# First layer of a two-block transformer stack: statistics of the tokens on VectorE at every second key unit, transposes inside the key units, no statistics on ScalarE, first copy in halves

## Chip, cores and metric

The kernel runs on one core of a Trainium2 chip. The metric is the device time of one execution in microseconds (us). "Before" and "after" are the two versions of the kernel. Times are medians of several executions, with the lowest and highest in brackets. A profile is one execution, and its span is about 1.8 us shorter than that execution's device time.

## The reference

Four layers on 2048 tokens of width 1024: linear attention (A), gated bilinear block (B), A, B, each on a layer norm of its input and added to it. Only the start of the first A layer matters here.

```python
def _A_ref(x, wqkv, wo):
    B, S, D = x.shape
    H = 32; Dh = D // H
    qkv = (x @ wqkv).reshape(B, S, 3, H, Dh).transpose(2, 0, 3, 1, 4)
    q, k, v = qkv[0], qkv[1], qkv[2]
    phi = lambda t: jnp.where(t > 0, t + 1, jnp.exp(t)) + 1e-6
    pq, pk = phi(q), phi(k)
    kv = jnp.einsum("bhsd,bhse->bhde", pk, v)
    z = jnp.einsum("bhsd->bhd", pk)
    # ... cut: num / den, times wo
x = A_x
x = x + _A_ref(_layernorm(x, axis=-1), A_wqkv, A_wo)
# ... cut: B, A, B in the same way
```

## The kernel before

The tokens are 16 tiles of 128, in four groups of four. For each tile the kernel takes mean and variance, normalises, transposes (the matmuls of this kernel read the tokens with D on the partitions), and runs two key units of eight 128x512 matmuls each. `phi` of a unit is one exponential on ScalarE and two passes on VectorE. The program emits each engine's instructions in the order of the calls below, and the traces show them run in that order (in after, an offset on Pool that was ready at 20.5 us ran at 22.88 us, behind one emitted earlier), so this order is the schedule. In the calls, `bn(t, h)` is `bn_stats` of half h of tile t, `ln_stats(t)` both halves and `moments(t)`, and `ln_apply(t, ...)` the normalisation, all on VectorE but for Pool's two steps in `moments`.

```python
def moments(t):                       # after two bn_stats of 512 columns each
    mv = small.tile([P, 2], F32, tag="mv", bufs=2 * TPG, name="mv")
    nc.vector.bn_aggr(out=mv[:], in_=stat[t][0][:])
    ve = small.tile([P, 1], F32, tag="ve", name="ve")
    nc.gpsimd.tensor_scalar(out=ve[:], in0=mv[:, 1:2], scalar1=1e-5, scalar2=None, op0=ALU.add)
    rstd = small.tile([P, 1], F32, tag="rstd", bufs=2 * TPG, name="rstd")
    nc.gpsimd.tensor_tensor(out=rstd[:], in0=ve[:], in1=mhalf[:], op=ALU.pow)
    stat[t] = (mv, rstd)

def ln_stats_act(t, xn):              # the same statistics by two ScalarE passes over the tile
    add = small.tile([P, 2], F32, tag="add", name="add")
    nc.scalar.activation(out=xn, in_=X[:, t, :], func=ACT.Identity, accum_out=add[:, 0:1])
    # ... cut: Pool makes -mean
    nc.scalar.activation(out=xn, in_=X[:, t, :], func=ACT.Square, bias=mv[:, 1:2], accum_out=add[:, 1:2])
    # ... cut: Pool makes mean, variance, rstd

def ln_apply_act(t, xn):
    mv, rstd = stat.pop(t)
    off = small.tile([P, 1], F32, tag="off", name="off")
    nc.gpsimd.tensor_scalar(out=off[:], in0=mv[:, 0:1], scalar1=rstd[:], scalar2=-1.0,
                            op0=ALU.mult, op1=ALU.mult)
    nc.scalar.activation(out=xn, in_=X[:, t, :], func=ACT.Identity, scale=rstd[:], bias=off[:])

def tx(xn, t, slot):                  # transpose by DMA
    tl = t % TPG
    nc.sync.dma_start_transpose(out=xT[slot][:, :, tl * P:(tl + 1) * P], in_=xn)

def tx_pe(xn, t):                     # transpose on TensorE, copy on ScalarE
    pt = psum.tile([P, KD, P], BF16, tag="mm", bufs=8, name="pt")
    for k in range(KD):
        nc.tensor.transpose(out=pt[:, k, :], in_=xn[:, k * P:(k + 1) * P], identity=ident[:])
    nc.scalar.copy(out=xT[t // TPG][:, :, t % TPG * P:(t % TPG + 1) * P], in_=pt[:])

def phi(ps, dst):
    e = work.tile([P, NB], BF16, tag="e", bufs=3, name="e")
    nc.scalar.activation(out=e[:], in_=ps[:], func=ACT.Exp)
    nc.vector.tensor_scalar(out=e[:], in0=e[:], scalar1=1.0, scalar2=1e-6, op0=ALU.min, op1=ALU.add)
    nc.vector.scalar_tensor_tensor(out=dst, in0=ps[:], scalar=1.0 + 1e-6, in1=e[:], op0=ALU.add, op1=ALU.max)

# first layer; k[2 * t + n] is the key unit of tile t, half n
def norm(t):
    ln_apply_act(t, xn_a[t])
    tx(xn_a[t], t, t // TPG)

bn(0, 0); bn(0, 1); moments(0)
bn(1, 0); ln_apply(0, xn_a[0]); tx_pe(xn_a[0], 0)
bn(1, 1); moments(1)
bn(2, 0); ln_apply(1, xn_a[1]); tx_pe(xn_a[1], 1)
bn(2, 1); moments(2)
bn(3, 0); ln_apply(2, xn_a[2])
bn(3, 1); moments(3); ln_stats(4)
k[0](); tx_pe(xn_a[2], 2); ln_apply(3, xn_a[3])
k[2](); tx_pe(xn_a[3], 3)
ln_stats_act(5, xn_a[5])
# ... cut: the rest of group 1, in the manner of the loop below
for g in range(2, NG):                # units of group g-1 with the norms of group g
    t = g * TPG
    u = k[8 * g - 8:8 * g]
    ln_stats(t)
    ln_stats_act(t + 1, xn_a[t + 1])
    u[0](); norm(t);     ln_stats(t + 2)
    u[1](); norm(t + 1); ln_stats(t + 3)
    u[2](); norm(t + 2)
    u[3](); norm(t + 3)
    do(u[4:])                         # ... cut: loads of input tiles 12 to 15 in between
do(k[8 * NG - 8:])
```

All matmul outputs rotate through eight PSUM buffers. Sixteen matmuls on zeros run while the first inputs arrive, to warm the clock up (in before's trace they take 634 ns each at first and 379 ns at the end).

## Time and profile before

| | before |
|---|---|
| device time | 1644.73 us (1644.15 to 1646.07, 3 runs); with a later fourth run 1644.59 |
| the profiled execution | 1646.92 us, span 1645.1 |
| TensorE busy | 1629.4 us, 99% |
| first key unit, first unit of tile 4, end of key units | 9.45, 28.59, 79.04 us |
| from the end of the key units to the end | 1566.06 us |

The first lines are of the page of before. The second line has busy time, share of the span and number of instructions per engine; the third has the granted TensorE clock in 40 equal slices, in tenths.

```profile
span 1645.1 us, 18292 instructions
...
PE 1629.4 (99%) x7696; PEld 744.8 (45%) x7696; DVE 641.3 (39%) x1042; ACT 270.4 (16%) x452; POOL 57.7 (4%) x159
...
PEclk9999999999999999999999999999999999999999
```

At this scale there is nothing to see: 16 us are idle in 1645, and a clock that was half for some 7 us does not show in a slice of 41 us. The timeline of TensorE of before does show it. Columns: start in us, length in us, engine, line, operation, output and inputs, count; in brackets the idle time before and what ended it. L214 is the transposes, L233 the key units.

```profile
9.45 1.89 PE L233 MATMUL ps<-W_74,xT_70 128*128 128x512 bf16 x8
14.19 0.62 PE L214 MATMUL pt<-ident,W_76 128*128 128x128 bf16 x8 [2.85 <-DVE W_76 L194]
...
17.77 0.62 PE L214 MATMUL pt<-ident,W_76 128*128 128x128 bf16 x8 [1.23 <-DVE W_76 L194]
...
44.76 1.90 PE L233 MATMUL ps<-W_74,xT_72 128*128 128x512 bf16 x8 [2.20 <-DMA xT_72<-XW]
...
62.81 3.59 PE L233 MATMUL ps<-W_74,xT_73 128*128 128x512 bf16 x8 [4.07 <-DMA xT_73<-D_84]
66.20 2.64 PE L233 MATMUL ps<-W_75,xT_73 128*128 128x512 bf16 x8
68.68 1.89 PE L233 MATMUL ps<-W_74,xT_73 128*128 128x512 bf16 x8
...
79.04 1.03 PE L245 MATMUL ps<-H,W_76 128*128 128x512 bf16 x4
```

A unit starts 1.727 us after the one before it when nothing waits. Three kinds of hole stand out: a start in which TensorE waits for VectorE's normalisation, a hole of 2.2 us before group 2 and one of 4.1 us before group 3. After the last, two units are slow. The stretches of before say why (columns: stretch, length, TensorE busy and count, granted clock, DMA share, GB/s):

```profile
62.00:64.00 2.00, 1.19 (x3) 0.50 0.10 18
64.00:66.00 2.00, 2.00 (x6) 0.50 0.68 131
66.00:68.00 2.00, 2.00 (x6) 0.57 0.68 131
68.00:70.00 2.00, 2.00 (x11) 1.00 1.00 165
```

The clock was half. It had fallen at about 60.9 us (the stretches 60.50:61.00 and 61.00:61.50 show 0.89 and 0.50). The timeline of ScalarE of before shows what made group 2 late. L180 and L183 are the two statistics passes of tile 9, L223 an exponential, L203 a normalisation.

```profile
33.07 1.07 ACT L180 ACTIVATE XW<-X 128x1024 bf16<-128x1024 bf16 x1
34.02 0.21 ACT L180 ACTIVATION_READ_ACCUMULATOR XW<-X 128x1 f32 x1
37.88 1.15 ACT L183 ACTIVATE XW<-X,mv 128x1024 bf16<-128x1024 bf16 x1 [3.65 <-POOL mv L182]
...
39.03 0.58 ACT L223 ACTIVATE e<-ps 128x512 bf16<-128x512 f32 x1
40.34 1.24 ACT L203 ACTIVATE XW<-X,off,rstd 128x1024 bf16<-128x1024 bf16 x1 [0.73 <-POOL off L201]
```

ScalarE stood still for 3.65 us between the two passes. The step of Pool that it waited for (L182) was in Pool's queue behind the variance of tile 8 (L167), which VectorE had not finished:

```profile
36.65 0.23 POOL L167 TENSOR_SCALAR ve<-mv 128x1 f32<-128x1 f32 x1 [7.56 <-DVE mv L165]
...
37.62 0.23 POOL L182 TENSOR_SCALAR mv<-add 128x1 f32<-128x1 f32 x1
```

The exponential at 39.03 us, for which VectorE waited 3.1 us, could not pass.

### The profile page before, as it was taken

The numbers are of one execution on the slowest core, as the hardware profiler recorded it, in microseconds if no ns is written. First come the engines' busy times: TensorE is split into PE (matmuls) and PEld (weight loads), VectorE is DVE, ScalarE is ACT, GpSimd is POOL, SyncE is SP. The second block draws the span as 40 slices with busy tenths as digits, with TensorE's granted clock in tenths as the row PEclk, the third lists the DMA queues.
The fourth block names the chain that finished last, engine by engine and source line by source line (L and its number), as shares of the span: only waits on it lengthen the run. The fifth ranks groups of instructions, "written<-read, shape, count | busy, mean of one in ns | idle before, by whom it ended". The sixth has DMA issues, their size and how long they took to land.

```text
span 1645.1 us, 18292 instructions
## 1 busy us (share of the span) xinstructions
PE 1629.4 (99%) x7696; PEld 744.8 (45%) x7696; DVE 641.3 (39%) x1042; ACT 270.4 (16%) x452; POOL 57.7 (4%) x159
## 2 busy tenths in 40 slices
PE   8899999999999999999999999999999999999999
PEld 3344544444444444444444444444444444444444
DVE  5789963211321321111677889531132113211111
ACT  4522301100110110011023223011011101100110
POOL 2100000000000000000200000000000000000000
PEclk9999999999999999999999999999999999999999
DMA  5602719630641363041460126394225406421400
GB/s 166 167 14 39 199 34 316 194 102 2 178 154 51 101 175 109 0 154 51 103 154 1 32 60 165 105 330 154 67 68 173 157 23 172 151 75 63 154 4 23
DMA packets 245009, 182.58 MB, mean 111 GB/s; under 512 B 100544, under 2 KB 235712, under 8 KB 244928
## 3 DMA queue, kind: packets, MB, share of 16 engines
q1 hardware_dynamic: 244928, 181.43, 38.2%
q8 instruction: 60, 0.98, 0.2%
q14 instruction: 21, 0.17, 0.0%
HBM read 153.09 MB, written 4.19 MB: 96 GB/s over the span
## 4 chain that ended last, share of the span: by engine, by line
PE 96%; DVE 1%; issue 1%; DMA 1%; ACT 1%; POOL 0%; SPq 0%; ACTq 0%; DVEq 0%
PE ps L348 47%; PE ps L365 24%; PE ps L233 11%; PE ps L334 7%; PE ps L245 7%; DVE H L225 0%; DMA X<-in_A_x_dram 0%; PE ps L310 0%; PE ps L319 0%; DVE st L161 0%; SPq L103 0%; ACT e L223 0%; DMA xT_73<-D_84 0%; DVE e L224 0%; POOL rstd L169 0%
## 5 line engine op out<-in xcount | busy, mean ns | idle before, releaser
L352 DVE TENSOR_TENSOR H<-gs,ps 128x512 bf16<-128x512 f32 x224 | 154.1, 688 | 575.1 <-PE ps L348 570.6
L351 ACT COPY gs<-ps 128x512 f32<-128x512 f32 x224 | 131.3, 586 | 1039.4 <-PE ps L348 1039.4
L365 PEld LDWEIGHTS <-H 128*128 128x128 bf16 x1848 | 178.5, 98 | 208.7
L367 DVE TENSOR_TENSOR X<-X,ps 128x512 bf16<-128x512 bf16 (+1 forms) x66 | 44.3, 671 | 319.7 <-PE ps L365 319.7
L223 ACT ACTIVATE e<-ps 128x512 bf16<-128x512 f32 x128 | 75.5, 595 | 164.7 <-PE ps L233 157.3
L348 PEld LDWEIGHTS <-W_75 128*128 128x128 bf16 x640 | 62.6, 98 | 75.5
L348 PEld LDWEIGHTS <-W_74 128*128 128x128 bf16 x640 | 62.6, 98 | 75.5
L348 PEld LDWEIGHTS <-W_77 128*128 128x128 bf16 x576 | 56.4, 98 | 67.9
L348 PEld LDWEIGHTS <-xT_73 128*128 128x128 bf16 x576 | 56.4, 98 | 67.9
L348 PEld LDWEIGHTS <-W_76 128*128 128x128 bf16 x576 | 56.4, 98 | 68.0
L348 PEld LDWEIGHTS <-xT_72 128*128 128x128 bf16 x576 | 56.4, 98 | 68.0
L161 DVE BATCH_NORM_STATS2 st<-X 128x6 f32<-128x512 bf16 x122 | 77.5, 675 | 5.7 <-DMA X<-in_A_x_dram 5.7
L348 PE MATMUL ps<-xT_71,W_74 128*128 128x512 bf16 x320 | 75.6, 379 | 0.0
L348 PE MATMUL ps<-xT_70,W_74 128*128 128x512 bf16 x320 | 75.6, 379 | 0.0
L348 PE MATMUL ps<-xT_71,W_75 128*128 128x512 bf16 x320 | 75.6, 379 | 0.0
L348 PE MATMUL ps<-xT_70,xT_73 128*128 128x512 bf16 x320 | 75.6, 379 | 0.0
L348 PE MATMUL ps<-xT_71,W_76 128*128 128x512 bf16 x320 | 75.6, 379 | 0.0
L348 PE MATMUL ps<-xT_71,W_77 128*128 128x512 bf16 x320 | 75.6, 379 | 0.0
L348 PE MATMUL ps<-xT_70,W_75 128*128 128x512 bf16 x320 | 75.6, 379 | 0.0
L348 PE MATMUL ps<-xT_70,xT_72 128*128 128x512 bf16 x320 | 75.6, 379 | 0.0
L365 PE MATMUL ps<-D_80,H 128*128 128x512 bf16 (+2 forms) x264 | 66.0, 373 | 0.0
L365 PE MATMUL ps<-D_78,H 128*128 128x512 bf16 (+2 forms) x264 | 66.0, 373 | 0.0
(125 smaller groups left out, 1825.7 us busy)
## 6 DMA issues: line engine op xcount, KB each, us to landing
W_74<-in_B_w_gate_dram SPq DMA_DIRECT2D x20, 1024.0 KB, 5.2
W_75<-in_B_w_up_dram SPq DMA_DIRECT2D x20, 1024.0 KB, 7.4
W_76<-in_B_w_gate_dram SPq DMA_DIRECT2D x18, 1024.0 KB, 5.2
W_77<-in_B_w_up_dram SPq DMA_DIRECT2D x18, 1024.0 KB, 7.0
xT_72<-in_B_w_gate_dram SPq DMA_DIRECT2D x18, 1024.0 KB, 5.2
xT_73<-in_B_w_up_dram SPq DMA_DIRECT2D x18, 1024.0 KB, 7.2
X<-in_A_x_dram SPq DMA_DIRECT2D x16, 256.0 KB, 4.9
H<-in_A_wo_dram SPq DMA_DIRECT2D x4, 1024.0 KB, 7.2
```

What stands on the lines that cost most here:

```text
L161: nc.vector.bn_stats(out=stat[t][0][:, c, :], in_=X[:, t, c * NB:(c + 1) * NB])
L223: nc.scalar.activation(out=e[:], in_=ps[:], func=ACT.Exp)
L233: nc.tensor.matmul(out=ps[:], lhsT=xt[:, k, tl * P:(tl + 1) * P], rhs=w[:, k, :], start=(k == 0), stop=(k == KD - 1))
L245: nc.tensor.matmul(out=ps[:], lhsT=xn_a[t][:, j * P:(j + 1) * P], rhs=pk[t][:, n * NB:(n + 1) * NB], start=(t == 0), stop=(t == NT - 1))
L334: nc.tensor.matmul(out=ps[:], lhsT=xT[t // TPG][:, c, tl * P:(tl + 1) * P], rhs=KVo[n][:, c, :], start=(c == 0), stop=(c == KD - 1))
L348: nc.tensor.matmul(out=ps[:], lhsT=w[:, k, j * P:(j + 1) * P], rhs=xT[g % 2][:, k, :], start=(k == 0), stop=(k == KD - 1))
L351: nc.scalar.copy(out=gs[:], in_=gp[:])
L352: nc.vector.tensor_tensor(out=hT[:, f, :], in0=gs[:], in1=up[:], op=ALU.mult)
L365: nc.tensor.matmul(out=ps[:, 0:hi - lo], lhsT=hT[:, f, tl * P:(tl + 1) * P], rhs=wd[f][:, cols], start=(f == 0), stop=(f == KF - 1))
L367: nc.vector.tensor_tensor(out=X[:, t, cols], in0=X[:, t, cols], in1=ps[:, 0:hi - lo], op=ALU.add)
```

## The change

The intent: statistics on VectorE only, one tile per two units, early enough that the DMA transposes land before their units; the transposes of tiles 1 to 3 inside units, so that TensorE does not wait for the copies; input tiles 3 to 11 loaded at once; first copy in two halves, so that the first four matmuls start earlier; three warm-up matmuls fewer. Cut to its core (`k_mm(t, n, ...)` emits the matmuls of one key unit and returns what `phi` needs; `txp(t)` is the transposes of tile t, which `mid` puts inside a unit):

```diff
-    for t in range(3, 2 * TPG):
+    for t in range(3, 3 * TPG):
         load_x(t)
-    for i in range(16):
+    for i in range(13):
         nc.tensor.matmul(out=zps[:], ...)
-    def ln_stats_act(t, xn): ...           # cut: dropped
-        nc.scalar.copy(out=xT[t // TPG][:, :, ...], in_=pt[:])
+        parts = 2 if t == 0 else 1
+        for ks in (slice(i * KD // parts, (i + 1) * KD // parts) for i in range(parts)):
+            nc.scalar.copy(out=xT[t // TPG][:, ks, ...], in_=pt[:, ks, :])
-    def proj(t, w, dst):
+    def proj_mm(t, w, mid=None, at=KD // 4):
         for k in range(KD):
+            if k == at and mid is not None:
+                mid()                      # the next tile's transposes
             nc.tensor.matmul(out=ps[:], ...)
-            # cut: the order of before's first layer
+            bn(0, 0); bn(0, 1); moments(0)
+            bn(1, 0); bn(1, 1); ln_apply(0, xn_a[0]); tx_pe(xn_a[0], 0)
+            moments(1); bn(2, 0); ln_apply(1, xn_a[1])
+            bn(2, 1); moments(2)
+            u = k_mm(0, 0, txp(1))
+            ln_apply(2, xn_a[2]); phi(*u)
+            u = k_mm(1, 0, txp(2))
+            ln_stats(3); bn(4, 0); ln_apply(3, xn_a[3]); bn(4, 1); moments(4)
+            phi(*u)
+            ln_apply(4, xn_a[4]); tx(xn_a[4], 4, 1)
+            units = [(2, 0), (0, 1), (1, 1), (3, 0), (2, 1), (3, 1)]
+            units += [(t, n) for t in range(TPG, NT) for n in range(2)]
+            ready = []
+            for i, (t, n) in enumerate(units):
+                u = k_mm(t, n, txp(3), KD // 2) if i == 1 else k_mm(t, n)
+                late = ready
+                ready = [4 + (i + 4) // 2 if i > 1 else 5 + i] if i < 2 or (i % 2 == 0 and i <= 18) else []
+                for x in ready:
+                    ln_stats(x)
+                phi(*u)
+                for x in late:
+                    norm(x)
+                if i == 2:
+                    for x in range(3 * TPG, NT):
+                        load_x(x)
```

## The prediction

> **What bounds the kernel.** The page gives TensorE 1629.4 us busy of 1645.1 (99%); the chain that ended last is TensorE for 96%. The list of TensorE's waits holds 12.8 us, all before 63 us. The timeline shows where: 1.2, 2.9 and 1.2 us before the transposes of tiles 1, 2, 3 (behind VectorE's normalisation), 2.2 us at 42.6 us and 4.1 us at 58.7 us (behind the DMA transposes of groups 2 and 3). After the 4.1 us hole the stretches show a granted clock of 0.50 until about 67.5 us: two units took 3.39 and 2.48 us instead of 1.73, 2.4 us more. The Trainium skill, "TensorE: Matmul & The Clock Gate", Part 1, says that an idle window of about 3.4 us halves the clock; holes of 2.9 (no drop) and 4.1 us (drop) agree.
>
> The 32 key units need 32 x 1.727 = 55.3 us; they end at 79.0 us. So 23.8 us of this stage is start, transposes, holes and slow clock. From there on TensorE never waits.
>
> **What the change does.**
> - VectorE no longer runs tile 3's statistics (input lands at 12.97 us) ahead of normalising tile 2. That was the 2.9 us hole.
> - Statistics on ScalarE go for three tiles: 1.06 + 0.19 + 1.15 + 0.19 us each, plus Pool steps between. Behind them VectorE waited 3 us for an exponential at 36.5 and 54.7 us. VectorE gets three more statistics (1.5 us each).
> - Statistics are spread one per two units: 1.51 + 2 x 0.93 = 3.37 us of VectorE per 3.45 us of TensorE.
> - Transposes of tiles 1 to 3 stand inside units, so ScalarE's 1.01 us copies hide. The first copy in halves lets the first unit start about 0.45 us earlier. Three warm-up matmuls go (they ended at 7.3 us, after tile 0 was ready at 6.6).
>
> **Walk with trace durations (estimate).** Tile 0 normalised 6.7, transposed 7.3, half copied 7.9, first unit 8.0. Tile 1 ready 8.9 (its apply stands behind tile 2's arrival, 7.66): wait 0.5, unit ends 10.7. Second unit, wait 0.2, ends 13.1; third 14.8. Fourth waits 0.4 for tile 3 (input 12.97, normalised 16.0), ends 17.4. From there units run back to back: tile 4 is needed at 24.3, lands 21.5; tile 5 27.8 against 25.5; tile 7 34.7 against 31.5 to 33; later ones 4 us or more to spare. VectorE lags TensorE by up to 6 us (3 to 4 units), within eight PSUM buffers, and catches up after the last statistics near 52 us. Key units end near 65.7 us instead of 79.0: 13.3 us off the critical path. 1644.7 - 13.3 = 1631.4; I add 0.4 for small slips.
>
> **Time:** 1631.8 us, 8 in 10 within 1628.5 to 1637. Faster by over 2%: 0.01; within 2%: 0.98; slower: 0.01.
>
> **What would show it.** No TensorE wait over 1 us after 10 us; clock 1.00 after warm-up; the first matmul of the next stage (line 245 before) near 65.7 us; VectorE about 97% busy from 18 to 52 us with phi 5 to 6 us behind its unit; everything later unchanged, 13 us earlier.
>
> **What would make it wrong.** VectorE is nearly full: 2 us more lag and the DMA transposes of tiles 4, 5, 7 come late and open holes again. Thirteen warm-ups may not release the clock: in the trace they sped up only near 5.9 us; then the first units run at half clock, about 2 us more.

## More of the kernel before

All ordinary loads and DMA transposes are issued by SyncE, in program order.

Tile 8's own offset, whose inputs were ready at 37.53 us, stood in Pool's queue behind tile 9's steps and ran at 40.04; so ScalarE normalised tile 8 at 40.34 us, its transpose was issued at 41.60, and TensorE got it at 44.76.

## The result, and the profile after

After takes 1634.24 us (1633.99 to 1634.62, 4 runs); before, in the same rounds and its earlier ones, 1644.59 us. The ratio is 0.9936, with a 95% interval of 0.9919 to 0.9953. The gain is 10.4 us.

The same lines of the page of after:

```profile
span 1632.4 us, 18134 instructions
...
PE 1618.0 (99%) x7543; PEld 743.6 (46%) x7693; DVE 645.2 (40%) x1052; ACT 262.2 (16%) x440; POOL 57.0 (3%) x152
...
PEclk9999999999999999999999999999999999999999
```

The trace of after has 7543 matmul records where 7693 weight loads ran; some matmul records are missing, so TensorE's busy time of the two pages is not compared. The timeline of TensorE of after (L199 the transposes, L222 the key units, L240 the next stage; adjoining units are merged):

```profile
1.17 4.77 PE L153 MATMUL zps<-xT 128*128 128x512 bf16 x13 [1.17 <-DVE xT L150]
...
8.00 0.60 PE L222 MATMUL ps<-W,xT 128*128 128x512 bf16 x2 [0.68 <-ACT xT L202]
...
11.37 4.05 PE L222 MATMUL ps<-W,xT 128*128 128x512 bf16 x17
15.75 0.62 PE L199 MATMUL pt<-ident,W 128*128 128x128 bf16 x8 [0.33 <-DVE W L179]
16.21 18.44 PE L222 MATMUL ps<-W,xT 128*128 128x512 bf16 x82
35.47 31.04 PE L222 MATMUL ps<-W,xT 128*128 128x512 bf16 x141 [0.82 <-DMA xT<-W]
66.56 1.89 PE L240 MATMUL ps<-H,W 128*128 128x512 bf16 x8
```

The big holes are gone. One new wait is left, 0.82 us at 35.47 us, for the DMA transpose of tile 7. Tile 4's first unit starts at 23.98 us (16.21 us plus half a unit plus four units of 1.727), 4.6 us earlier than before. The key units end at 66.56 us, 12.5 us earlier. What follows takes 1565.84 us, against 1566.06: nothing was given back later.

Yet the timed medians are only 10.4 us apart. The profiled execution of before took 1646.92 us, 2.3 us above its median; that of after, 1634.15 us, lies on its median. So 2.1 us of the 12.5 are a question about the kernel before, and the wait for tile 7 is a question about the kernel after.

Two traces bear on the second. First, Pool in after: L167 and L169 are the variance steps of a tile, L186 the offset with which ScalarE normalises it.

```profile
19.61 0.22 POOL L167 TENSOR_SCALAR ve<-mv 128x1 f32<-128x1 f32 x1 [2.11 <-DVE mv L165]
19.91 0.57 POOL L169 TENSOR_TENSOR rstd<-ve,mhalf 128x1 f32<-128x1 f32 x1
21.93 0.22 POOL L167 TENSOR_SCALAR ve<-mv 128x1 f32<-128x1 f32 x1 [1.45 <-DVE mv L165]
22.23 0.57 POOL L169 TENSOR_TENSOR rstd<-ve,mhalf 128x1 f32<-128x1 f32 x1
22.88 0.27 POOL L186 TENSOR_SCALAR off<-mv,rstd 128x1 f32<-128x1 f32 x1
```

Tile 5's inputs were ready at 20.5 us, but its offset ran at 22.88: the program emits it after tile 6's statistics, so it stood behind tile 6's variance, which waited for VectorE. The Trainium skill ("Perfetto Trace Analysis", section "Per-engine timelines", in the note on TensorE) says that ScalarE, VectorE and GpSimd run strictly in order of arrival; this trace agrees, with 2.4 us lost. Second, the issues of SyncE in after (L193 a DMA transpose, L103 a load):

```profile
18.11 10.06 SPq L193 DMA_TRANSPOSE xT<-W  x3
28.22 2.00 SPq L103 DMA_DIRECT2D X<-in_A_x_dram  x4
30.33 1.39 SPq L193 DMA_TRANSPOSE xT<-W  x1
```

Tile 7 was normalised at 28.5 us. Its transpose was issued at 30.33, behind four loads of 256 KB, and landed 5.1 us later (the chain of waits), where transposes of this stage usually took 3.1.

### The profile page after: what moved, and what is told of

It reads as the page before. It is cut to its first block, busy times and chain, and to the rows that moved or that the text cites. A ratio compares the mean times of both kernels' runs of the same rounds, so it can differ in the third digit from the quotient of the medians.

```text
span 1632.4 us, 18134 instructions
## 1 busy us (share of the span) xinstructions
PE 1618.0 (99%) x7543; PEld 743.6 (46%) x7693; DVE 645.2 (40%) x1052; ACT 262.2 (16%) x440; POOL 57.0 (3%) x152
## 4 chain that ended last, share of the span: by engine, by line
PE 97%; DMA 1%; issue 1%; DVE 1%; SPq 0%; POOL 0%; ACT 0%; ACTq 0%
PE ps L343 47%; PE ps L360 24%; PE ps L222 12%; PE ps L240 7%; PE ps L329 7%; DMA X<-in_A_x_dram 0%; PE ps L305 0%; PE ps L314 0%; SPq L103 0%; DMA xT<-W 0%; DVE st L161 0%; PE ps L266 0%; POOL rstd L169 0%; DVE H L212 0%; ACT e L210 0%
## 5 line engine op out<-in xcount | busy, mean ns | idle before, releaser
L343 PE MATMUL ps<-xT,W 128*128 128x512 bf16 x2380 | 525.8, 379 | 2.8
L360 PE MATMUL ps<-D,H 128*128 128x512 bf16 (+2 forms) x1811 | 385.9, 372 | 1.8
L343 PEld LDWEIGHTS <-W 128*128 128x128 bf16 x2432 | 238.0, 98 | 286.9
L343 PE MATMUL ps<-xT,xT 128*128 128x512 bf16 x1134 | 250.6, 379 | 1.0
L343 PEld LDWEIGHTS <-xT 128*128 128x128 bf16 x1152 | 112.7, 98 | 135.9
L222 PEld LDWEIGHTS <-xT 128*128 128x128 bf16 x1024 | 99.6, 98 | 121.7 <-DMA xT<-W 2.0
L222 PE MATMUL ps<-D,xT 128*128 128x512 bf16 x501 | 114.8, 379 | 0.5
L222 PE MATMUL ps<-W,xT 128*128 128x512 bf16 x501 | 110.9, 379 | 2.0 <-DMA xT<-W 0.8
L329 PE MATMUL ps<-D,xT 128*128 128x512 bf16 x502 | 110.3, 379 | 0.5
L329 PEld LDWEIGHTS <-xT 128*128 128x128 bf16 x512 | 50.1, 98 | 60.4
L240 PE MATMUL ps<-H,W 128*128 128x512 bf16 x248 | 59.9, 379 | 0.5
L167 POOL TENSOR_SCALAR ve<-mv 128x1 f32<-128x1 f32 x64 | 15.0, 234 | 1295.9 <-DVE mv L165 1295.9
L321 DVE TENSOR_TENSOR X<-X,ps 128x512 bf16<-128x512 bf16 x64 | 42.1, 679 | 32.8 <-PE ps L329 32.8
L212 DVE SCALAR_TENSOR_TENSOR pq<-ps,e 128x512 bf16<-128x512 f32 x64 | 44.3, 692 | 2.5
```

The source lines that it names most:

```text
L222: nc.tensor.matmul(out=ps[:], lhsT=xt[:, k, tl * P:(tl + 1) * P], rhs=w[:, k, :], start=(k == 0), stop=(k == KD - 1))
L240: nc.tensor.matmul(out=ps[:], lhsT=xn_a[t][:, j * P:(j + 1) * P], rhs=pk[t][:, n * NB:(n + 1) * NB], start=(t == 0), stop=(t == NT - 1))
L321: nc.vector.tensor_tensor(out=X[:, t, n * NB:(n + 1) * NB], in0=X[:, t, n * NB:(n + 1) * NB], in1=ps[:], op=ALU.add)
L329: nc.tensor.matmul(out=ps[:], lhsT=xT[t // TPG][:, c, tl * P:(tl + 1) * P], rhs=KVo[n][:, c, :], start=(c == 0), stop=(c == KD - 1))
L343: nc.tensor.matmul(out=ps[:], lhsT=w[:, k, j * P:(j + 1) * P], rhs=xT[g % 2][:, k, :], start=(k == 0), stop=(k == KD - 1))
L360: nc.tensor.matmul(out=ps[:, 0:hi - lo], lhsT=hT[:, f, tl * P:(tl + 1) * P], rhs=wd[f][:, cols], start=(f == 0), stop=(f == KF - 1))
```

## The experiments

Theory A, on the kernel before: the half clock behind the hole of group 3 is not in every execution, so the profile held a cost of some 2 us that the usual run does not pay. Its rival B: the half clock is always there and the 2 us are noise of profiling. Theory C, on the kernel after: the wait for tile 7 comes from the four loads ahead of its transpose in SyncE's queue; its rival D: tile 7 was normalised too late for another reason, of which Pool's order is one (experiment 7). Besides, the gain is to be split into its parts: dropping ScalarE's statistics, spreading, the new front.

Experiments 1 to 4 ran on one chip, 5 to 8 on a second, 9 to 12 on a third, each set with nine runs of before in between.

### 1. The kernel before again

No edit.

> The kernel before, unchanged, to see its own spread. Theory A (the half clock after the 4.1 us hole comes in some executions only): the runs fall into two groups about 2.4 us apart, one near 1644.3 us with mean granted clock 1.000, one near 1646.7 us with 0.998; each run's clock tells which. Rival B (the hole always costs the half clock, and the gap between the 12.7 us of the two profiles and the 10.4 us of the timed medians is profiling or chip noise): all runs have clock 0.998 and differ without relation to the clock.

Measured: 1644.80 us (1644.35 to 1644.89, 5 runs); the profiled execution took 1644.85. TensorE of this run:

```profile
45.68 15.67 PE L233 MATMUL ps<-W,xT 128*128 128x512 bf16 x63 [2.77 <-DMA xT<-XW]
63.14 13.99 PE L233 MATMUL ps<-W,xT 128*128 128x512 bf16 x62 [1.78 <-DMA xT<-D]
```

Its stretches behind the two holes (columns as above):

```profile
46.00:48.00 2.00, 2.00 (x6) 0.50 0.68 131
...
64.00:66.00 2.00, 1.95 (x10) 1.00 0.68 131
```

This execution had its half clock behind the hole of group 2, where it made the eight units take 15.67 us instead of 13.99. That cost nothing: group 3 waits for its DMA transposes anyway, and only its hole became shorter. Behind group 3's hole the clock was 1.00, and from there to the next stage it took 13.8 us (63.14 to 76.96), where the first profiled execution took 16.2 (62.81 to 79.04). The key units end at 76.96 us instead of 79.04: 2.1 us earlier, and the run was 2.1 us shorter. Theory A holds for these two executions, and rival B, by which the half clock always follows the hole of group 3, does not. The two groups of runs that A expected did not show here: all five lie within 0.6 us (of the nine runs of before beside them, one took 1646.32 us). Its expectation about the mean clock falls: 0.998 stands beside 1644.85 us as well as beside 1646.9, because a mean does not tell where the clock fell. Against 66.56 us in after, 76.96 is 10.4 us, which is the gain of the medians.

### 2. Before, with matmuls in the hole before group 3

```diff
@@ -452,2 +452,5 @@
                 do(u[4:])
+            keep = mm_tile()
+            for i in range(10):
+                nc.tensor.matmul(out=keep[:], lhsT=xT[0][:, 0, 0:P], rhs=xT[0][:, 0, :], start=True, stop=True)
             do(k[8 * NG - 8:])
```

> The kernel before with ten idle matmuls (2.2 us, read by nothing) at the head of the hole before group 3, so that the hole that is left is about 2 us. Theory A: every run has clock 1.000 and lies near 1644.3 us, the slower group is gone; the first units of group 3 take 1.73 us each in the trace. Rival B: all runs drop by 2.4 us, to about 1642.1. If the matmuls themselves stood in the way, it would be slower.

Measured: 1645.46 us (1644.43 to 1646.29); before 1644.86. Neither theory's number. The added matmuls took a PSUM buffer of their own and shifted the rotation: the trace has a new wait of 0.50 us for VectorE to free a buffer, at 67.27 us. In the profiled execution the clock was 1.00 in groups 2 and 3. This shows that the half clock of experiment 1 in group 2 was free: here too group 2 starts at 45.68 us, its units take 13.99 us instead of 15.67, and group 3 still starts at 63.14 us, because the DMA transposes were issued at 60.05 us here and at 60.04 there. Rival B asked for 1642.1 us, and no run came below 1644.4; that speaks against B. The spread was not settled by this run.

### 3. Before, with ScalarE's statistics on VectorE and nothing else

```diff
@@ -415,3 +415,3 @@
             tx_pe(xn_a[3], 3)
-            ln_stats_act(5, xn_a[5])
+            ln_stats(5)
             norm(4)
@@ -437,3 +437,3 @@
                     load_x(13)
-                ln_stats_act(t + 1, xn_a[t + 1])
+                ln_stats(t + 1)
                 u[0]()
```

> The kernel before with the statistics of tiles 5, 9 and 13 moved from ScalarE to VectorE, nothing spread. If the two ScalarE passes and their Pool steps are what makes groups 2 and 3 late: the hole of 2.2 us before group 2 closes and that before group 3 shrinks to under 1 us, the clock does not drop, the time is near 1639 us (5 to 6 us less than before). If the spreading is what matters (four tiles of statistics in a row still make VectorE late): holes of 2 us and more stay, time 1642 to 1644.

Measured: 1640.45 us (1639.73 to 1644.39); before 1644.86; a gain of 4.4 us by the medians. The hole before group 2 closed. The hole before group 3 did not: 2.50 us of waiting for the DMA transpose are left. The offset of tile 12 was done at 54.6 us, its own statistics at 51.9, with tile 13's variance in front of it in Pool's queue. Its inputs were ready at 52.8 us, so Pool's order held it back by 1.6 us here too. Dropping ScalarE's passes thus brings 4.4 of the 7.8 us that experiment 5 gains, a little less than the 5 to 6 us expected. Whether spreading or Pool's order alone would close the rest is not shown: this kernel was not run with the offset earlier. The one run of 1644.39 us had a mean clock of 0.997; there is no trace of it.

### 4. After's front with before's groups 2 and 3

The first six units and tiles 0 to 7 as in after, with its early loads; then before's loop over groups 2 and 3.

```diff
             units = [(2, 0), (0, 1), (1, 1), (3, 0), (2, 1), (3, 1)]
-            units += [(t, n) for t in range(TPG, NT) for n in range(2)]
-                ready = [...] if i < 2 or (i % 2 == 0 and i <= 18) else []
+                ready = [...] if i < 3 else []
+            for g in range(2, NG):      # before's loop, with ln_stats_act
+                ...
```

> After's first part (tiles 0 to 7 and their units, inputs loaded early) with the groups 2 and 3 of before. In the two traces the first unit of tile 4 starts at 28.59 and 23.98 us, 4.6 us apart. If gains add: near 1644.4 - 4.6 = 1639.8 us. If VectorE's greater lag in this front (its phi some 7 us behind, against 6) is carried into group 2: the hole before group 2 grows by about 1 us and the time is near 1641 us; the hole before group 3 stays at about 4 us, and the clock may drop in some runs.

Measured: 1642.21 us (1641.43 to 1643.70); before 1644.86. That is a gain of 2.7 us, less than either number. TensorE of this run:

```profile
40.34 13.99 PE L237 MATMUL ps<-W,xT 128*128 128x512 bf16 x63 [1.27 <-DMA xT<-XW]
58.34 16.24 PE L237 MATMUL ps<-W,xT 128*128 128x512 bf16 x62 [4.01 <-DMA xT<-D]
```

Group 3 starts 4.8 us earlier than in experiment 1 (58.34 against 63.14), so the front's gain did arrive. But the hole before it is 4.0 us here, and behind it, with 0.50 of the clock granted at first, it took 16.3 us to the next stage (58.34 to 74.64) instead of 13.8. The key units end at 74.64 us, 2.3 us earlier than in experiment 1 (76.96); the medians gave 2.7.

### 5. Before's front with after's spread

The loop of after for units 3 to 29 in place of before's loop over groups 2 and 3; the front as in before.

```diff
-            do(k[5:8])
-            for g in range(2, NG):      # before's loop
-                ...
+            ready = []
+            for i in range(3, 30):
+                late = ready
+                ready = [4 + (i + 4) // 2] if 4 <= i <= 18 and i % 2 == 0 else []
+                t, n = (i - 3 + 5) // 2, (i - 3 + 5) % 2
+                u = k_mm(t, n)
+                for x in ready:
+                    ln_stats(x)
+                phi(*u)
+                for x in late:
+                    norm(x)
+                if i == 5:
+                    for x in range(3 * TPG, NT):
+                        load_x(x)
```

> Before's first part (tiles 0 to 7, their order and their input loads) with after's spread statistics for tiles 8 to 15. The traces give 50.45 us from the first unit of tile 4 to the end of the key units before, 42.58 us after, 41.4 us if nothing waits; 2.4 us of before's is the half clock that the usual run does not have. So without holes: 50.45 - 2.4 - 41.4 = 6.6 us gain, near 1637.8 us, clock 1.000. If a late front starves it, some hole stays before tile 8 and it is 1639 to 1641.

Measured: 1637.55 us (1637.08 to 1638.21); before 1645.35 on this chip; a gain of 7.8 us. TensorE ran from 18.44 us to the end of the key units in one piece:

```profile
18.44 51.96 PE L233 MATMUL ps<-W,xT 128*128 128x512 bf16 x240
```

The expectation held. This part alone is three quarters of the gain, and it comes with little spread: there is no hole in groups 2 and 3 and no half clock. (The front kept its hole of 2.86 us, with half clock behind it: the unit at 15.04 us took 3.12 us.) The gains of experiments 4 and 5, each against before on its own chip, sum to 10.5 us; the change brought 10.4. That they add up is partly luck: the profiled execution of experiment 4 paid 2.5 us of half clock that after does not pay, and the medians of before on the two chips differ by 0.5 us.

### 6. After, with the late loads one unit later

```diff
@@ -427,3 +427,3 @@
                     norm(x)
-                if i == 2:
+                if i == 3:
                     for x in range(3 * TPG, NT):
```

> After, with the four loads of input tiles 12 to 15 issued one unit later, behind tile 7's transpose. Theory C (the remaining 0.8 us wait, 1.1 us of start of tile 7's first unit, comes from these loads ahead of the transpose in the same queue and on the same DMA engines: issue at 30.33 where tile 7 was normalised at 28.5, landing 5.1 us later instead of 3.1): that wait is gone and the time is 1633.1 us, 1.1 less than after. Rival D (tile 7 was normalised too late for another reason): the wait stays, time 1634.2.

Measured: 1633.38 us (1632.97 to 1633.96). The wait before tile 7 is gone from the trace: its transpose was issued at 28.3 us and landed 3.1 us later, not 5.1. Theory C holds; the gain is 0.9 us against the 1634.24 of after, measured on another chip.

### 7. After, with Pool's offset earlier

```diff
@@ -181,5 +181,4 @@
 
-    def ln_apply_act(t, xn):
-
-        mv, rstd = stat.pop(t)
+    def ln_off(t):
+        mv, rstd = stat[t]
         off = small.tile([P, 1], F32, tag="off", name="off")
@@ -187,2 +186,8 @@
                                 op0=ALU.mult, op1=ALU.mult)
+        stat[t] = (mv, rstd, off)
+
+    def ln_apply_act(t, xn):
+        if len(stat[t]) == 2:
+            ln_off(t)
+        mv, rstd, off = stat.pop(t)
         nc.scalar.activation(out=xn, in_=X[:, t, :], func=ACT.Identity, scale=rstd[:], bias=off[:])
@@ -422,2 +427,4 @@
                 ready = [4 + (i + 4) // 2 if i > 1 else 5 + i] if i < 2 or (i % 2 == 0 and i <= 18) else []
+                for x in late:
+                    ln_off(x)
                 for x in ready:
```

> After, with Pool's offset for a tile emitted ahead of the next tile's statistics. In after's trace the offset of tile 5 stands behind the variance step of tile 6 in Pool's order: ready at 20.5, done at 23.15. Expected: ScalarE normalises tile 5 near 21 instead of 23.2 us, tile 6 near 23.5 instead of 25.7, VectorE's two waits for exponentials (0.8 and 1.5 us near 24 to 27 us) go; tile 7 is normalised near 26 instead of 27.3, its transpose issues near 28 and lands near 33, in time for 34.3: time 1633.1, like the run with late loads. If Pool's order does not matter: 1634.2.

Measured: 1633.20 us (1632.85 to 1633.31). Pool and SyncE of this run:

```profile
20.20 0.57 POOL L169 TENSOR_TENSOR rstd<-ve,mhalf 128x1 f32<-128x1 f32 x1
20.87 0.27 POOL L185 TENSOR_SCALAR off<-mv,rstd 128x1 f32<-128x1 f32 x1
22.20 0.22 POOL L167 TENSOR_SCALAR ve<-mv 128x1 f32<-128x1 f32 x1 [1.07 <-DVE mv L165]
```

```profile
26.03 2.00 SPq L103 DMA_DIRECT2D X<-in_A_x_dram  x4
28.13 1.48 SPq L198 DMA_TRANSPOSE xT<-W  x1
```

The offset of tile 5 now runs at 20.87 us, ahead of tile 6's variance. ScalarE normalises tile 5 at 21.17 us (23.18 in after), VectorE's two waits are gone, and tile 7's transpose is issued 2.2 us earlier although the loads still stand before it. The wait is gone too, although the transpose still took 5.1 us to land behind the loads. The slip in Pool's order was thus the other half of the same cause: with either one mended, tile 7 is in time.

### 8. Both

Both edits above.

> After with both edits (late loads, early offset). The wait can be removed only once: 1633.1 us, the same as either alone, not 1632.0. No TensorE wait left after 16 us.

Measured: 1633.47 us (1632.84 to 1633.60): no better than either alone, as expected of one wait that can be removed once.

### 9. The kernel after again

No edit.

> The kernel after, unchanged, on the chip of the three runs beside it: near 1634.2 us, clock 1.000 in every run, so that the edits can be compared on one chip.

Measured: 1634.41 us (1633.64 to 1634.58), clock 1.000 in every run; before on this chip 1644.81 us. The wait for tile 7 is there again, 0.90 us. All five runs of experiment 7 lie below all nine of after, though on another chip; the confidence intervals of the ratios to before (0.9926 and 0.9934) overlap, so the times alone would not decide it.

### 10. Before, with matmuls in the hole, in a buffer that is free

```diff
@@ -227,2 +227,4 @@
 
+    warmed = []
+
     def proj(t, w, dst):
@@ -231,2 +233,6 @@
         xt, tl = xT[t // TPG], t % TPG
+        if (t, w is wk[0]) == (3 * TPG, True) and not warmed:
+            warmed.append(1)
+            for i in range(12):
+                nc.tensor.matmul(out=ps[:], lhsT=xT[0][:, 0, 0:P], rhs=xT[0][:, 0, :], start=True, stop=True)
         for k in range(KD):
```

> The kernel before with twelve matmuls (2.6 us) in the hole before group 3, written into the PSUM buffer that the next unit overwrites anyway, so that the rotation of buffers stays as it was. Theory A in its mended form (the half clock can strike after any of before's three holes; after the first two it is absorbed by the next hole, which ends with a DMA transpose, and only behind the hole of group 3 does it cost up to 2.4 us): no run above 1645.2 us, all within 1644.3 to 1645.2, while about a third of the runs of the kernel before lie above 1645.5. Rival B: runs above 1645.5 stay as frequent.

Measured: 1644.62 us (1644.31 to 1645.67). Two of five runs lie above 1645.2, so the expectation did not hold as written. The profiled execution is the slowest of them:

```profile
45.89 15.67 PE L239 MATMUL ps<-W,xT 128*128 128x512 bf16 x63 [2.22 <-DMA xT<-XW]
61.40 2.75 PE L237 MATMUL ps<-xT 128*128 128x512 bf16 x11
63.99 13.98 PE L239 MATMUL ps<-W,xT 128*128 128x512 bf16 x63
```

Group 2 ran at half clock in this execution, the hole behind it was short, and the added matmuls filled it to the brim and beyond: group 3 started without any wait at 63.99 us, where 63.14 had been possible in experiment 1. Its eight units took 13.98 us, the clock stayed up. No run reached 1646, while three of the nine runs of before beside it did (1646.02 to 1647.03). That fits theory A, but five runs are few. Over all 36 timed runs of before, 26 lie between 1643.9 and 1645.2 and eight between 1646.0 and 1647.6. That all eight had their half clock in group 3 is not shown: only two of the executions of before have a trace.

### 11. After, with the first copy whole and sixteen warm-ups

```diff
@@ -151,3 +151,3 @@
     zps = psum.tile([P, NB], F32, tag="mm", bufs=8, name="zps")
-    for i in range(13):
+    for i in range(16):
         nc.tensor.matmul(out=zps[:], lhsT=xT[3][:, 0, 0:P], rhs=xT[3][:, 0, :], start=True, stop=True)
@@ -199,3 +199,3 @@
             nc.tensor.transpose(out=pt[:, k, :], in_=xn[:, k * P:(k + 1) * P], identity=ident[:])
-        parts = 2 if t == 0 else 1
+        parts = 1
         for ks in (slice(i * KD // parts, (i + 1) * KD // parts) for i in range(parts)):
```

> After with the first copy whole again and sixteen warm-up matmuls. The first unit then starts about 0.5 us later, but TensorE waits 0.33 us for tile 3 (input at 12.6 us) a few units later anyway. If that wait absorbs it: 0.0 to 0.2 us slower than after. If the earlier start is worth its 0.45 us: 1634.7.

Measured: 1634.08 us (1634.05 to 1634.61), against 1634.41 of after on the same chip. The first unit starts at 8.33 us, and nothing of it is left at the end: tile 3 (its wait is 0.81 us in this run) absorbs it. The wait for tile 7 is there in this execution too. The view of TensorE's matmuls puts the late start at 35.46 us to VectorE, with 0.32 us; the weight load of the same unit, at 35.46 us too, waited 0.81 us for the DMA transpose. These two parts of the change are worth nothing that can be measured here.

### 12. Early offset, and input tile 3 loaded before the second half of the weights

The edit against experiment 7:

```diff
@@ -130,5 +130,6 @@
             load_x(2)
+    load_x(3)
     for k in range(0, KD, 4):
         load(wk[1][:, k:k + 4, :], wqkv_v[:, k:k + 4, D + NB:2 * D])
-    for t in range(3, 3 * TPG):
+    for t in range(4, 3 * TPG):
         load_x(t)
```

> The early-offset kernel with the load of input tile 3 issued ahead of the second half of the weights. Tile 3 would land near 9.7 instead of 12.6 us and the 0.3 to 0.8 us wait before its transposes goes; the weights land near 13 us and are needed at 14.5. Expected 0.4 us faster than the early-offset kernel: 1632.8 us. If the weights come late instead, 1633.2 or more.

Measured: 1632.51 us (1632.31 to 1632.66), 1.9 us faster than after on the same chip, with no overlap of the runs, and 12.3 us faster than before there (ratio 0.9924, 0.9912 to 0.9937). TensorE of this run:

```profile
15.29 0.62 PE L205 MATMUL pt<-ident,W 128*128 128x128 bf16 x8
15.75 49.16 PE L228 MATMUL ps<-W,xT 128*128 128x512 bf16 x223
...
64.96 1.89 PE L246 MATMUL ps<-H,W 128*128 128x512 bf16 x8
```

The transposes of tile 3 no longer wait, and the rest runs in one piece. The key units end at 64.96 us, 1.6 us earlier than in after. Against experiment 7 (1633.20 us, on another chip) tile 3's earlier load brings 0.7 us where 0.4 was expected. This version beats both kernels.

## Why the prediction was right or wrong, point by point

- **What bounds the kernel, and where the time lies: right.** All the gain was in the first 79 us. The rest took 1565.84 us against 1566.06.
- **The walk through the front: right to a few tenths.** First unit predicted at 8.0 us, measured 8.00; tile 4's first unit 24.3 and 23.98. Worth in the end 4.6 to 4.8 us, if no half clock takes part of it back (experiments 4 and 5).
- **"Key units end near 65.7 us instead of 79.0: 13.3 us off the critical path. 1644.7 - 13.3 = 1631.4": this is the step that failed, by the size of one term.** The 13.3 us were counted on the profiled execution, and they hold 2.4 us of half clock; they were then taken off the median of timed runs, most of which do not pay it. The profiled execution was 1646.92 us long, 2.3 above that median. The measured end of the key units, 66.56 us, is 12.5 us before that execution's, and 10.4 us before that of the execution in experiment 1. The difference between 1644.7 and 1646.9 stood in the numbers before the prediction was made.
- **"Tile 7 34.7 against 31.5 to 33": wrong, by a mechanism that the walk left out.** It landed at 35.4 us, and TensorE lost 1.1 us: 24 units from 23.98 us would have ended at 65.4 instead of 66.56. The walk names no step of Pool between a tile's statistics and its normalisation; in Pool's order the offset of tile 5 waited for the next tile's (experiment 7), and the loads before the transpose made up the rest (experiment 6). The risk "2 us more lag and the DMA transposes of tiles 4, 5, 7 come late" named the tile.
- **VectorE: right in kind, off in size.** From 18 to 52 us it was busy for 30.6 of 34 us, 90%, not 97%, and phi of tile 4's first unit ended 8.4 us after the unit, not 5 to 6. With Pool's order mended (experiment 7) VectorE was busy for 32.7 of 34 us, 96%, and phi ended 5.9 us after: the forecast describes that kernel.
- **The halved copy: the first unit did start earlier, but the walk itself shows a wait of 0.4 us for tile 3 after it.** Experiment 11 found no value in it.
- **The clock with thirteen warm-ups: the risk did not come true.** In after the first eight key matmuls in a row (at 8.99 us) took 1.89 us, the length at full clock, and so in every trace with thirteen warm-ups (after again and experiments 4, 6 to 8 and 12). The clock of 1.000 in all nine runs of after does not tell: the record reads 1.00 also from 1 to 3 us of after, where the warm-up matmuls took 634 ns against 379 later.
- The sum, in us, by the traces: 12.5 measured, less 2.3 that only the slow execution pays, is 10.2; the medians gave 10.4. Predicted were 12.9 (1644.7 - 1631.8). Or from the 1631.4 of the walk: 2.2 for the execution that it was counted on (1646.9 against 1644.7) and 0.9 for the end of the key units (66.56 against 65.7) make 1634.5; measured were 1634.24.

## What to carry to other kernels

Before a difference is counted on one profiled execution, compare that execution's own time with the median of the timed runs; a half clock behind a hole can sit in one and not in the other, and it costs only if no later wait absorbs it. When two engines feed each other through a third that runs strictly in order, walk the third one's queue as well: here a step of 0.27 us on Pool, emitted one tile too late, cost ScalarE 2 us and, with four loads ahead of a transpose, TensorE one. Parts of a change that start something earlier are worth nothing as long as the next wait ends with an input that comes at a fixed time.

## What the Trainium skill lacked or had wrong

- "TensorE: Matmul & The Clock Gate", Part 1, has the clock halved after at least one idle window of about 3.4 us, a window that runs freely. The traces show less regularity below that: holes of 2.75 us (before 14.2 us) and 2.77 us (before 45.7 us) in experiment 1 and of 2.22 us (before 45.9 us) in experiment 10 were followed by half clock, while holes of 2.85 and 2.20 us in before and one of 2.77 us in experiment 2 were not. In before's hole of 4.07 us the clock fell after 2.1 us. A hole shorter than 3.4 us is thus not safe.
- No page that I read tells that a half clock can be free: in experiment 1 it lengthened eight units by 1.68 us, from 13.99 to 15.67, and the next wait gave it back; behind the last hole the same thing cost 2.1 us.
- No page that I read gives the time to landing of a DMA transpose behind loads of the same queue: a 128x1024 bf16 transpose took 3.1 us by the median of the stage in after, and tile 7's 5.1 us behind four loads of 256 KB (3.1 us ahead of them, in experiment 6).
